# Splitting a 2048-point column transform as 32x64 in place of 16x128, inside a TensorE-bound kernel

## Chip, cores and metric

The kernel runs on one core of one Trainium2 chip. The metric is device time in microseconds (us) of that core, as the median of several executions. The kernel before took 1284.75 us (three runs, 1283.58 to 1288.89).

## The reference, cut to what matters

The kernel computes the output below and the gradients of eight of its inputs (nine outputs in all).

```python
def _A_ref(x, w_r, w_i):                      # S = 2048, D = 1024, Df = 513
    X = jnp.fft.rfft2(x.astype(jnp.float32), axes=(-2, -1))
    X = X * (w_r + 1j * w_i)
    return jnp.fft.irfft2(X, s=(S, D), axes=(-2, -1)).astype(jnp.bfloat16)

def _B_ref(x, w1, b1, w2, b2):                # F = 3584
    r = relu(einsum("bsd,df->bsf", x, w1) + b1)
    return einsum("bsf,fd->bsd", r * r, w2) + b2

g = sigmoid((x * gate_w).sum(-1, keepdims=True))
out = g * _A_ref(x, ...) + (1 - g) * _B_ref(x, ...)
# and the vector-Jacobian product with grad_out, for everything but B_x
```

Two real sequences go through the two-dimensional transform together: `x` and the gradient that flows into the spectral branch (index `T` in the code). The rest is matmuls of the MLP in bf16.

## The kernel before

The two-dimensional transform is a side job. Its generators `yield` after a piece of work, and a helper threads these pieces between groups of 16 MLP matmuls, so that TensorE always has something to do. In the traces TensorE runs its matmuls in one fixed order: while one waits (4.65 us in the step shown below), none of those behind it passes.

The transform over the 2048 rows is split in two factors, and the longer one is what the change rewrites. Before, it is a 128-point stage: a complex product with a 128x128 matrix, done as three real products (the third one on the sum of the two parts), with the common term added afterwards. This is the forward half of a step, for one of the two sequences:

```python
def spectrum(fb, m, z, mats, x):
    # ... pm = sums and differences of z; sums = re + im   (VectorE)
    for j in range(2):
        re, im = main[j]
        px = fps.tile([P, 2, H], FP32, ...)            # PSUM, H = 512
        ps = tps.tile([P, H], FP32, ...)               # PSUM
        mm(px[:, 0, :], lhsT=mats[:, j, 1, :], rhs=im, ...)
        mm(px[:, 1, :], lhsT=mats[:, j, 2, :], rhs=re, ...)
        mm(ps[:],       lhsT=mats[:, j, 0, :], rhs=sums[:, j], ...)
        common = fb.tile([P, H], FP32, ...)
        nc.scalar.copy(                                 # L328
            out=common[:].rearrange("p (i g) -> p i g", g=4),
            in_=ps[:].rearrange("p (g i) -> p i g", g=4))
        V(out=x[:, j, :, 0:H].rearrange("p c (i g) -> p c i g", g=4),        # L331
          in0=px[:].rearrange("p c (g i) -> p c i g", g=4),
          in1=common[:]..."p (o i g) -> p o i g"..., op=ALU.add)
        yield
```

The two rearranged views undo an ordering: column `g*128+i` of PSUM goes to column `i*4+g` of `x`.

The way back (`back`) has the same three products with a second matrix, ScalarE's copy of the common term, and additions on VectorE. Between the two stand the products with the spectral weights `w`. Each of the 8 steps covers a pair of the 16 long-row transforms.

Of the kernel before, what the change touches and what calls it, by code (L numbers as in the profile page):

```python
# [10 lines left out]
P = 128  # L11
# [9 lines left out]

class Geo:

    def __init__(self, S, D, F):
        assert S % P == 0 and D % P == 0 and F % P == 0
        self.S, self.D, self.F = S, D, F
        self.S2 = S // P
        assert P % self.S2 == 0
        self.Df = D // 2 + 1
        self.DC = D // P  # L30
        self.DW = min(512, D)
        assert D % self.DW == 0
        self.DCH = D // self.DW
        self.FC = F // P
        self.FGW = 512 if F % 512 == 0 else F
        assert F % self.FGW == 0 and self.FGW % P == 0
        self.FG = F // self.FGW
        self.FGC = self.FGW // P
        self.SB = 4
        assert self.S2 % self.SB == 0  # L40
        self.NSB = self.S2 // self.SB


def build_consts(g: Geo):
# [8 lines left out]
    t, pl = q // 8, q % 8  # L53
    same = (pl[:, None] == pl[None, :]).astype(np.float64)

    cc = np.arange(16)
    k2 = np.where(cc <= 8, cc, cc - 8)
    ang = tp * ((np.arange(16)[:, None] * k2[None, :]) % 16) / 16
    kf = np.where(cc[None, :] <= 8, np.cos(ang), -np.sin(ang))
    c["kf"] = (kf[t][:, t] * same).astype(FDT_NP)  # L60
    ki = np.where(cc[None, :] <= 8, np.cos(ang), np.sin(ang)).T
    c["ki"] = (ki[t][:, t] * same).astype(FDT_NP)
# [30 lines left out]
    pp = np.arange(P)  # L93
    A = np.zeros((P, S2, 3, P))
    B = np.zeros((P, S2, 3, P))
    for k in range(S2):
        th = tp * ((pp[:, None] * (k + S2 * pp[None, :])) % S) / S
        A[:, k, 0, :], A[:, k, 1, :], A[:, k, 2, :] = np.cos(th), np.sin(th) - np.cos(th), -np.cos(th) - np.sin(th)
        th = th.T
        B[:, k, 0, :], B[:, k, 1, :], B[:, k, 2, :] = np.cos(th), np.sin(th) - np.cos(th), -np.cos(th) - np.sin(th)  # L100
    c["amat"] = (A * XS).astype(FDT_NP)
    c["apmat"] = B.astype(FDT_NP)
    c["sel"] = np.tile(np.eye(32, dtype=np.float32), (4, 1))
    sg = np.ones((P, 2, 2, 2))
    sg[:, 1, 1, :] = -1.0
    c["sgn"] = sg.astype(np.float32)
# [20 lines left out]
def kernel(  # L127
# [30 lines left out]
    S2, DC, FC = g.S2, g.DC, g.FC  # L158
    NT = S // P
# [31 lines left out]
    kf = pers.tile([P, P], FDT, name="kf", tag="kf")  # L191
# [10 lines left out]
    z_scr = [dram.tile([S2, P, D], FDT, name=f"z_scr{T}") for T in range(2)]  # L202
    y_scr = [dram.tile([S2, P, D], FDT, name=f"y_scr{T}") for T in range(2)]
# [40 lines left out]
    def row_stage(fb, f, kmat, earlier=None):  # L244
# [3 lines left out]
        for b, (row, o) in enumerate(even + odd):  # L248
            first_ = mm(pk[:, b, :], lhsT=f[:, row, o], rhs=kmat, start=True, stop=True)
# [6 lines left out]
    def first_columns(fb, cf, T, i, ft, earlier=None):  # L256
# [6 lines left out]
        nc.scalar.copy(  # L263
            out=u[:].rearrange("p (h b r) -> p b h r", h=2, b=2)[:, 0], in_=pu[:, 0, :].rearrange("p (h r) -> p h r", h=2)
        )

        uv = u[:].rearrange("p (g c i) -> p g c i", g=4, c=2)
        X, Y = (w[:, :, x].rearrange("p c g i -> p g c i") for x in range(2))
        V(out=uv[:, 1::2, :, 0 : P // 2], in0=X, in1=Y, op=ALU.add)
        V(out=uv[:, 3::-2, :, P - 1 : P // 2 - 1 : -1], in0=X, in1=Y, op=ALU.subtract)  # L270
        st(out=z_scr[T][:].rearrange("c (p i) l -> i (c p) l", i=S2)[i], in_=u[:])
# [18 lines left out]
    def pair(m):  # L290
        return (m, S2 - m) if m else (0, S2 // 2)

    def rows2(ap, m):
        ka, kb = pair(m)
        return ap.rearrange("(k1 k2) l -> k1 k2 l", k2=S2)[:, ka : kb + 1 : kb - ka, :]

    def pair_mats(fb, name, m):
        ka, kb = pair(m)
        t_ = fb.tile([P, 2, 3, P], FDT, name=name, tag=name, bufs=2)
        ld(out=t_[:], in_=cten[name].ap()[:, ka : kb + 1 : kb - ka])  # L300
        return t_

    def zg(ap):
        return ap.rearrange("p (g c i) -> p c g i", g=4, c=2)

    def spectrum(fb, m, z, mats, x):

        if m:
            pm = fb.tile([P, 4, 4, P], FDT, name="pm", tag="pm")
            R, I = zg(z[:, 0]), zg(z[:, 1])[:, ::-1]  # L310
            V(out=pm[:, 2:0:-1], in0=R, in1=I, op=ALU.add)
            V(out=pm[:, 0::3], in0=R, in1=I, op=ALU.subtract)
            main = [(pm[:, 0], pm[:, 1]), (pm[:, 2], pm[:, 3])]
            re_, im_ = pm[:, 0::2], pm[:, 1::2]
        else:
            main = [(zg(z[:, j])[:, 0], zg(z[:, j])[:, 1]) for j in range(2)]
            re_, im_ = (z.rearrange("p j (g c i) -> p c j g i", g=4, c=2)[:, c] for c in range(2))
        sums = fb.tile([P, 2, 4, P], FDT, name="sums", tag="sums", bufs=2)
        V(out=sums[:], in0=re_, in1=im_, op=ALU.add)
        for j in range(2):  # L320
            re, im = main[j]
            px = fps.tile([P, 2, H], FP32, name="px", tag="ps2", bufs=2)
            ps = tps.tile([P, H], FP32, name="pxs", tag="tr", bufs=2)
            mm(px[:, 0, :], lhsT=mats[:, j, 1, :], rhs=im, start=True, stop=True)
            mm(px[:, 1, :], lhsT=mats[:, j, 2, :], rhs=re, start=True, stop=True)
            mm(ps[:], lhsT=mats[:, j, 0, :], rhs=sums[:, j], start=True, stop=True)
            common = fb.tile([P, H], FP32, name="common", tag="common", bufs=2)
            nc.scalar.copy(  # L328
                out=common[:].rearrange("p (i g) -> p i g", g=4), in_=ps[:].rearrange("p (g i) -> p i g", g=4)
            )  # L330
            V(  # L331
                out=x[:, j, :, 0:H].rearrange("p c (i g) -> p c i g", g=4), in0=px[:].rearrange("p c (g i) -> p c i g", g=4),
                in1=common[:].rearrange("p (o i g) -> p o i g", o=1, g=4).to_broadcast([P, 2, P, 4]), op=ALU.add,
            )
            yield

    def real_columns(fb, m, z, mats, xs, sgn):

        ed = fb.tile([P, 2, 2, 2, 2], FDT, name="ed", tag="ed", bufs=2)
        zc = z[:].rearrange("p t c l -> p c t l")[:, :, :, 0 : P + 1 : P]  # L340
        G = nc.gpsimd
        sp = tps.tile([P, 2, 2, 4], FP32, name="sp", tag="tr", bufs=2)
        if m:

            G.tensor_tensor(out=ed[:, 0, 0], in0=zc[:, 0], in1=zc[:, 1], op=ALU.add)
            G.tensor_tensor(out=ed[:, 0, 1], in0=zc[:, 1], in1=zc[:, 0], op=ALU.subtract)
            G.tensor_copy(out=ed[:, 1, 0], in_=zc[:, 1])
            G.tensor_scalar(out=ed[:, 1, 1], in0=zc[:, 0], scalar1=-1.0, scalar2=None, op0=ALU.mult)
            src = [[ed[:, a].rearrange("p c t l -> p (c t l)") for a in range(2)]] * 2
        else:  # L350

            ed0 = fb.tile([P, 2, 4, 4], FDT, name="ed0", tag="ed0")
            G.memset(ed0[:], 0.0)
            G.tensor_copy(out=ed0[:, :, 0, :].rearrange("p j (t l) -> p j t l", t=2), in_=zc)
            for a in (1, 3):
                G.tensor_scalar(
                    out=ed0[:, :, a, :].rearrange("p j (t l) -> p j t l", t=2), in0=zc, scalar1=-1.0, scalar2=None, op0=ALU.mult
                )
            src = [[ed0[:, j, a : a + 2, :].rearrange("p a b -> p (a b)") for a in (0, 2)] for j in range(2)]
        for j in range(2):  # L360
            o = sp[:, j].rearrange("p c b -> p (c b)")
            mm(o, lhsT=mats[:, j, 0, :], rhs=src[j][0], start=True, stop=False, skip_group_check=True)
            mm(o, lhsT=mats[:, j, 1 + j, :], rhs=src[j][1], start=False, stop=True, skip_group_check=True)
        for T in range(2):
            V(out=xs[T][:, :, :, 0::H], in0=sp[:, :, :, 2 * T : 2 * T + 2], in1=sgn[:], op=ALU.mult)

    def back(fb, m, ys, mats):

        vs = []
        for T in range(2):  # L370
            y = ys[:, T]
            v = fb.tile([P, 2, 2, LW], FDT, name="v", tag="v", bufs=2)
            sums = fb.tile([P, 2, H], FDT, name="ysums", tag="sums", bufs=2)
            V(out=sums[:], in0=y[:, :, 0, 0:H], in1=y[:, :, 1, 0:H], op=ALU.add)
            for j in range(2):
                pv = fps.tile([P, 2, H], FP32, name="pv", tag="ps2", bufs=2)
                ps = tps.tile([P, H], FP32, name="pvs", tag="tr", bufs=2)
# [37 lines left out]
    def fft_mid():  # L415
# [4 lines left out]
        def inputs(m):  # L420
            z = fb.tile([P, 2, 2, D], FDT, name="z", tag="z", bufs=2)
            for T in range(2):
                ld(out=z[:, T], in_=z_scr[T][:].rearrange("c p l -> p c l")[:, m : m + 9 : 8, :])
# [847 lines left out]
```

## Time and profile before

The prediction below shows the busy shares, two waits, the windows over the stage and its timeline. The stage is recognised in the trace by its neighbours:

| first start, us | kernel before |
|---|---|
| first MLP gradient matmul (`pw`), start of the stage | 446.1 |
| first `pki`, the way back over the rows begins | 790.3 |
| first `acc`, the stage is over | 893.6 |
| end of the profiled execution | 1283.3 |

### The profile page before, as it was taken

The numbers are of one execution on the slowest core, as the hardware profiler recorded it, in microseconds if no ns is written. First come the engines' busy times: TensorE is split into PE (matmuls) and PEld (weight loads), VectorE is DVE, ScalarE is ACT, GpSimd is POOL, SyncE is SP. The second block draws the span as 40 slices with busy tenths as digits, with TensorE's granted clock in tenths as the row PEclk, the third lists the DMA queues.
The fourth block names the chain that finished last, engine by engine and source line by source line (L and its number), as shares of the span: only waits on it lengthen the run. The fifth ranks groups of instructions, "written<-read, shape, count | busy, mean of one in ns | idle before, by whom it ended". The sixth has DMA issues, their size and how long they took to land.

```text
span 1283.3 us, 18045 instructions
## 1 busy us (share of the span) xinstructions
PE 1270.6 (99%) x6948; PEld 615.1 (48%) x6948; DVE 739.5 (58%) x1563; ACT 440.5 (34%) x736; POOL 187.0 (15%) x335
## 2 busy tenths in 40 slices
PE   8999999999999999999999999999999999999998
PEld 5555544555544444444444444555454454344443
DVE  3554433444481246686567854444877777886664
ACT  4656654666633323332333323443111121111110
POOL 0111111111100121221212222122010011000000
PEclk9999999999999999999999999999999999999999
DMA  9566353546344678898787589995899887656550
GB/s 290 199 181 183 130 156 124 180 150 193 105 129 118 158 233 194 242 214 222 180 178 180 132 151 277 292 214 185 221 217 225 197 202 207 174 152 177 149 154 33
DMA packets 314416, 234.20 MB, mean 182 GB/s; under 512 B 183852, under 2 KB 263754, under 8 KB 314330
## 3 DMA queue, kind: packets, MB, share of 16 engines
q1 hardware_dynamic: 284944, 142.19, 47.1%
q0 software_dynamic: 24576, 82.43, 18.7%
q10 hardware_dynamic: 4810, 8.43, 2.3%
q8 instruction: 54, 0.88, 0.3%
q14 instruction: 32, 0.26, 0.1%
HBM read 107.16 MB, written 81.81 MB: 147 GB/s over the span
## 4 chain that ended last, share of the span: by engine, by line
PE 60%; DVE 5%; DMA 2%; issue 2%; SPq 1%; POOL 1%; ACT 0%; POOLq 0%; DVEq 0%; ACTq 0%
PE pw L804 14%; PE acc L876 13%; PE pw L788 9%; PE xX L976 7%; PE xV L976 4%; PE pd L657 3%; PE ph L647 3%; PE xZ L976 2%; DMA z<-z_scr 2%; PE pui L282 1%; PE pki L503 1%; SPq L167 1%; DMA out_dram<-wo 1%; PE pvs L380 1%; PE pv L378 0%
## 5 line engine op out<-in xcount | busy, mean ns | idle before, releaser
L647 PE MATMUL ph<-xT,w1g 128*128 128x512 bf16 x896 | 221.1, 379 | 1.2 <-DMA w1g<-in_B_w_dram 1.2
L657 PE MATMUL pd<-dbT,w2T 128*128 128x512 bf16 x896 | 211.3, 379 | 0.4 <-DVE dhT L661 0.4
L804 PE MATMUL pw<-grp,res 128*128 128x512 bf16 x896 | 202.2, 379 | 0.0
L788 PE MATMUL pw<-dbn,grp 128*128 128x512 bf16 x896 | 201.1, 379 | 0.0
L876 PE MATMUL acc<-w,hblk 128*128 128x512 bf16 x896 | 198.7, 379 | 0.0
L661 DVE SCALAR_TENSOR_TENSOR dhT<-pd,rT 128x512 bf16<-128x512 f32 x112 | 77.4, 692 | 208.7 <-PE pd L657 156.4
L657 PEld LDWEIGHTS <-w2T 128*128 128x128 bf16 x896 | 87.1, 98 | 103.4 <-issue 1.2
L788 PEld LDWEIGHTS <-grp 128*128 128x128 bf16 x896 | 86.8, 98 | 102.6
L876 PEld LDWEIGHTS <-hblk 128*128 128x128 bf16 x896 | 86.4, 98 | 98.3
L804 PEld LDWEIGHTS <-res 128*128 128x128 bf16 x896 | 86.0, 98 | 97.8 <-issue 0.2
L647 PEld LDWEIGHTS <-w1g 128*128 128x128 bf16 x896 | 84.6, 98 | 90.4 <-DMA w1g<-in_B_w_dram 1.5
L649 ACT ACTIVATE rT<-ph,b1col 128x512 bf16<-128x512 f32 x112 | 76.9, 687 | 116.2 <-PE ph L647 116.2
L792 ACT CAST wo<-pw 128x512 bf16<-128x512 f32 x56 | 32.8, 585 | 140.3 <-PE pw L788 137.0
L809 ACT CAST wo<-pw 128x512 bf16<-128x512 f32 x56 | 32.8, 586 | 131.7 <-PE pw L804 97.1
L650 ACT ACTIVATE h2T<-rT 128x512 bf16<-128x512 bf16 x112 | 70.5, 629 | 2.5
L942 ACT ACTIVATE g<-gatew_bc,dsc 128x1024 f32<-128x1024 bf16 x16 | 18.3, 1148 | 150.7 <-DVE gxo L985 124.5
L976 PEld LDWEIGHTS <-dS 128*128 128x128 f16 x448 | 43.8, 98 | 52.8
L331 DVE TENSOR_TENSOR x<-px,common 128x1024 f16<-128x1024 f32 x32 | 38.8, 1220 | 48.8 <-ACT common L328 45.0
L505 ACT CAST rt<-pki 128x1024 f16<-128x1024 f32 x32 | 32.5, 1014 | 96.7 <-PE pki L503 88.7
L976 PEld LDWEIGHTS <-hblk 128*128 128x128 bf16 x336 | 33.1, 99 | 44.7 <-issue 3.3
L877 DVE SCALAR_TENSOR_TENSOR ot<-acc,omg,af 128x512 bf16<-128x512 f32 x32 | 24.0, 749 | 49.9 <-PE acc L876 49.7
L976 PE MATMUL xX<-dT,dS 128*128 128x512 f16 x224 | 51.0, 379 | 0.0
(201 smaller groups left out, 1517.7 us busy)
## 6 DMA issues: line engine op xcount, KB each, us to landing
h2T_scr<-h2T POOLq DMA_DIRECT2D x28, 512.0 KB, 4.4
dhT_scr<-dhT POOLq DMA_DIRECT2D x28, 512.0 KB, 4.8
hblk<-h2T_scr SPq DMA_DIRECT2D x8, 1792.0 KB, 9.8
hblk<-dhT_scr SPq DMA_DIRECT2D x8, 1792.0 KB, 8.7
z_scr<-u POOLq DMA_DIRECT2D x32, 256.0 KB, 2.9
z<-z_scr SPq DMA_DIRECT2D x16, 512.0 KB, 5.1
y_scr<-pc POOLq DMA_DIRECT2D x16, 512.0 KB, 6.5
r<-y_scr ACTq DMA_DIRECT2D x32, 256.0 KB, 4.8
```

The source lines that it names most:

```text
L331: V(out=x[:, j, :, 0:H].rearrange("p c (i g) -> p c i g", g=4), in0=px[:].rearrange("p c (g i) -> p c i g", g=4), in1=common[:].rearrange( ...
L647: mm(ph[:], lhsT=w1g[:, dc, fc % 2 * P : (fc % 2 + 1) * P], rhs=xT[:, dc, ss], start=(dc == 0), stop=(dc == DC - 1))
L649: nc.scalar.activation(rT[:], ph[:], ACT.Relu, bias=b1col[:, fc : fc + 1])
L650: nc.scalar.activation(h2T, rT[:], ACT.Square)
L657: mm(pd[:], lhsT=w_[:, ec, fc % FGC * P : (fc % FGC + 1) * P], rhs=dbT[:, ec, ss], start=(ec == 0), stop=(ec == DC - 1),)
L661: return STT(out=dhT, in0=pd[:], scalar=2.0, in1=rT[:], op0=ALU.mult, op1=ALU.mult, accum_out=gb1part[:, fc, sb : sb + 1],)
L788: mm(pw[:], lhsT=cur[:, t, fb_ * P : (fb_ + 1) * P], rhs=dbn[:, t, hf * H : (hf + 1) * H], start=(t == 0), stop=(t == NT - 1),)
L792: last = nc.scalar.copy(out=wo[:, hf * H : (hf + 1) * H], in_=pw[:])
L804: mm(pw[:], lhsT=xr[t][:, d_ * P : (d_ + 1) * P], rhs=cur[:, t, :], start=(t == 0), stop=(t == NT - 1),)
L809: nc.scalar.copy(out=wo[:], in_=pw[:])
L876: turn["PE"] = mm(acc[:], lhsT=cur[:, fc, t2 * P : (t2 + 1) * P], rhs=w2[:, fc, cs], start=(fc == 0), stop=(fc == FC - 1))
L976: mm(acc[:], lhsT=lhs[:, fc, :], rhs=rhs[:, fc, :], start=start and fc == 0, stop=fc == KH - 1, skip_group_check=True,)
```

## The change

The intent is to take matmuls out of a stream that TensorE bounds. With a factor of 64 in place of 128, a complex 64-point transform fits one 128x128 matrix with the real and the imaginary part stacked on the partitions: one matmul does what needed three, on half as many points. 192 matmuls of 512 columns become 128. The rest follows from this: 16 steps in place of 8, the edge columns (0 and 512) read once ahead of all steps, results that must be brought from the other 64 partitions, and weights `w` with a negated copy.

The core of the diff:

```diff
-    def spectrum(fb, m, z, mats, x):
-        ...three matmuls per j, common, V(...)   (shown above)
+        def transform(m, z):
+            if m:
+                pm = fb.tile([P, 2, 2, H], FDT, name="pm", tag="pm")
+                V(out=pm[:, 0], in0=z[:, 0], in1=z[:, 1], op=ALU.add)
+                V(out=pm[:, 1], in0=z[:, 0], in1=z[:, 1], op=ALU.subtract)
+            else:
+                pm = z
+            x = fb.tile([P, 2, 2, LW], FDT, name="x", tag="x", bufs=2)
+            for n in range(2):
+                px = fps.tile([P, 2, H], FP32, name="px", tag="ps2", bufs=2)
+                for T in range(2):
+                    mm(px[:, T, :], lhsT=am[:, m, n, :], rhs=pm[:, n, T, :], start=True, stop=True)
+                for c in range(2):
+                    nc.scalar.copy(
+                        out=x[lanes[n], c, :, 0:H].rearrange("p t (i g) -> p t g i", g=4),
+                        in_=px[lanes[c]].rearrange("p t (g i) -> p t g i", g=4),
+                    )
+                yield x
+        def products(x, w):
+            G.tensor_scalar(out=w[:, 2, 0:W1], in0=w[:, 1, 0:W1], scalar1=-1.0, ...)   # GpSimd
+            V(out=xw(t1_), in0=xw(x), in1=w[:, 0:1, 0:W1]..., op=ALU.mult)
+            V(out=t2_[...], in0=x[...], in1=wi, op=ALU.mult)
+            yield
+            for n in (1, 0):
+                V(out=y[lanes[0], n, ...], in0=t1_[L, 0, ...], in1=t2_[L, 1, ...], op=ALU.subtract)
+                V(out=y[lanes[1], n, ...], in0=t1_[L, 1, ...], in1=t2_[L, 0, ...], op=ALU.add)
+            yield y
+        def back(m, y):
+            for n in (1, 0):
+                for T in range(2):
+                    mm(pv[n][:, T, :], lhsT=bm[:, m, n, :], rhs=y[:, n, T, 0:H], start=True, stop=True)
+                # n == 1: ScalarE copies pv[1] to vc; n == 0: two sums on VectorE to pc
+                yield
+            # edges, stores of pc
+        for m in range(NM):                      # 16 steps
+            for x in transform(m, z):
+                yield
+            G.tensor_copy(out=x[:, :, :, 0::H], in_=ex[:, m])     # edge columns
+            for y in products(x, w):
+                yield
+            yield from back(m, y)
+            grads_of_w(m, x)
+            yield
```

## The prediction

> **What bounds the kernel now.** I read the page's busy shares first, then the 40 slices, then the waits of TensorE alone, then the windows over the stage that is rewritten, then its timeline and its groups with the shapes kept apart.
>
> ```profile
> PE 1270.6 (99%) x6948; PEld 615.1 (48%) x6948; DVE 739.5 (58%) x1563; ACT 440.5 (34%) x736; POOL 187.0 (15%) x335
> ...
> PEclk9999999999999999999999999999999999999999
> ...
> PE xX L976 <- DVE dT L971: 2.7, 1, 2.7
> PE ph L647 <- DMA w1g<-in_B_w_dram: 1.2, 1, 1.2
> ...
> 460.00:660.00 200.00, 199.30 (x956) 89.93 (x955) 137.72 (x196) 60.86 (x94) 44.40 (x85) 1.00 0.82 208
> 660.00:790.00 130.00, 129.72 (x622) 58.73 (x621) 84.52 (x125) 38.69 (x60) 30.37 (x59) 1.00 0.75 168
> ```
>
> The first line: TensorE is busy 99% of the span. A busy share alone can hide stalls, so the waits matter more: the nine entries of TensorE add up to 8.2 us, and the largest two (shown) lie at the tail and in the first stage. The windows (length, then busy time of PE, PEld, DVE, ACT, POOL, then clock, DMA share, GB/s) cover the middle of the two-dimensional transform, the stage that is rewritten: TensorE idles 0.70 us of 200 and 0.28 of 130. There the transform is a side job, threaded between groups of 16 matmuls of the MLP gradients (pw). So in this stage time is TensorE's instruction stream, and the change is worth what it takes out of that stream, less any wait it puts in.
>
> How long is a matmul in the stream? The 379 ns that the groups give is the latency of one; the timeline gives the pitch:
>
> ```profile
> 525.57 0.38 PE L378 MATMUL pv<-y,apmat 128*128 128x512 f16 x1
> 525.78 0.38 PE L379 MATMUL pv<-y,apmat 128*128 128x512 f16 x1
> 526.00 0.38 PE L380 MATMUL pvs<-ysums,apmat 128*128 128x512 f16 x1
> 526.21 3.62 PE L788 MATMUL pw<-dbn,grp 128*128 128x512 bf16 x16
> 529.67 0.38 PE L378 MATMUL pv<-y,apmat 128*128 128x512 f16 x1
> ...
> 513.81 0.17 PE L362 MATMUL sp<-ed,amat 128*128 128x8 f16 x1
> 513.84 0.17 PE L363 MATMUL sp<-ed,amat 128*128 128x8 f16 x1
> ```
>
> Starts go from 526.21 to 529.67 over 16 matmuls: 216 ns each; the three transform matmuls before them take 0.64 us, 213 ns each. So a 512-column matmul costs 0.216 us, with a new stationary operand every time; an 8-column one 0.03 us.
>
> [...]
>
> **The change part by part.** Before, the stage has 8 steps over pairs of the 16 long-row transforms. A complex product with real and imaginary parts apart is done with three real 128x128 matmuls; per step 2 inputs x 2 of the pair x 3 = 12 forward and 12 back, 24 x 8 = 192 matmuls of 512 columns. After, there are 16 steps over pairs of 32; one stationary 128x128 matrix does a complex 64-point transform of both parts, so per step 2 of the pair x 2 inputs = 4 forward and 4 back, 8 x 16 = 128. Removed: 64.
>
> TensorE: 64 x 0.216 = **13.8 us out**. Small edge matmuls: before 4 + 4 per step, 64; after 32 in one block at the start and 2 per step back, 64 again: 0. Row stage (kf, ki): 8 blocks of 128 columns per tile as before; only which half of the constant is the moving operand changes: 0. Column stage: unchanged. MLP: unchanged.
>
> VectorE, per new step: two sums for pm at 0.69 us (1.38), two products of 2052 elements at 1.24 (2.48), four combinations of 1026 elements at 0.69 (2.76; half the lanes cost no less), two sums from PSUM at 1.22 (2.44), edges 0.34, weight gradients 2 x 0.69 + 2 x 0.42 + 0.17 (2.39): 11.8 us, x16 = 189. Before, the rows of this stage (x 38.8, v 38.7, t 59, y 22, pm 19, pc 19, sums 21, gs 11, small ones 10) sum to some 240. About 50 us leave VectorE. ScalarE: four casts from PSUM of 1024 elements in each lane at 1.01 (the rt row's mean), one more for the way back, gw 0.96: 6.0 x 16 = 96 against 8 x (8 x 0.59 + 1.92) = 53; with the split cast in the first stage (two fixed costs of some 0.2 instead of one, x32 = 6) about 50 us more. Neither engine sets the end: ScalarE would be near 46% of a step (6.0 + 5.3 casts of wo at 0.59, over 20 us).
>
> GpSimd and queues: stores per 20 us step are 4 of y and 4 of gw, at the 0.72 to 0.73 of their rows some 6 us, plus about 2 for small copies and the negated weights: 8 of 20. SP issues 8 loads per step at about 0.45 (z's median issue): 3.6 us. The pair matrices go from 16 transfers of 192 KB to 2 of 1 MB. All this lies beside the matmuls.
>
> A step is now 7 pieces. The mixing rate goes from 129/110 to 145/110 side pieces per group, so a step spans 7/1.318 = 5.3 groups of 16, 5.3 x 3.45 + 8 x 0.216 + 0.1 = 20 us; 16 such are 322 us against the 8 x 41 = 330 of now. The stage keeps its place and ends some 8 us sooner; the rest of the 13.8 appears where the later pieces are mixed in. Sum: 1284.75 - 13.8 = **1271.0 us** without new waits.
>
> **Rivals.**
> *(1) The edge gather becomes a wait.* The new edges are read once, ahead of everything, from the scratch as single 2-byte elements: 8 transfers of 64 x 16 elements plus one of 64 x 4 = 8448 elements. The fast queue of now moved 284944 packets in 47.1% of 16 x 1283 us, 34 ns per packet; if elements cost as much, 8448 x 34 / 16 = 18 us, an estimate. They stand behind 2 MB of matrices (some 8 us at the 272 GB/s of this window), and the stage's loads start at 446.3, just as its MLP gradients do:
>
> ```profile
> 446.31 0.35 SPq L418 DMA_DIRECT2D sgn<-c_sgn  x1
> 446.70 0.94 SPq L423 DMA_DIRECT2D z<-z_scr  x2
> ...
> 456.48 0.38 PE L324 MATMUL px<-z,amat 128*128 128x512 f16 x1
> ```
>
> So the edges land near 475, while the first transform matmul stands at 456 and its edge matmuls at 473 now. If the 32 new edge matmuls are placed for an earlier landing, TensorE, which takes them in order, waits. For: nothing but pw covers it. Against: the order seen is not that of the source (one sums product is moved behind a pw matmul at 505.98), so placement follows expected readiness. I give one such wait of 5 to 15 us about one chance in four, which makes 1276 to 1286.
>
> *(2) The shorter step is too short for its chain.* From the last forward matmul to the first one back: two casts 2.0, edge copy 0.5, two products 2.5, two combinations 1.4, hops 0.7: 7 us, against three pieces, mostly two or three groups, 6.9 or 10.4 us. For: it is at the brink. Against: now the same chain has eight operations on VectorE (7.7 us by its rows) after 1.8 us of eviction, and TensorE waits 0.6 us in all (pvs, pv), because pw matmuls fill the gap. If it bites, 0.5 us in 16 steps, 8 us: 1279.
>
> *(3) GpSimd or the DMA becomes the bound.* Twice as many z and y row pieces of 1 KB in the outer stages, four times the stores per unit of time on GpSimd. Against: GpSimd 8 of 20 us. DMA is at 0.82 now; with buffers two deep a late z costs TensorE only if it is over 10 us late. I expect 0 to 3 us.
>
> *(4) Relief of VectorE pays more than the matmuls.* It can't: TensorE waited under 1 us for it in this stage. This caps the gain near 15 us, 1.2%.
>
> **Range and chances.** The expected waits are 0.25 x 9 for (1), and a little under 1 for (2) and (3), of which most is inside the rounding: +1.5 to +3 on 1271.0. I predict 1272.5 us. Low: all 64 matmuls and 1 us of old waits gone, 1270, less 3 for the spread of the runs before (1283.6 to 1288.9): 1267. High: a gather wait of the middle size or the chain's wait: 1283. Faster by over 2% would be below 1259.1, twice what the matmuls hold: 0.02. Slower by over 2% would be above 1310, some 39 us of new waits, more than the gather's estimate twice over: 0.03. Within 2%: 0.95.
>
> **What would show it right or wrong.** Right: TensorE's matmuls go from 6948 to about 6884, its busy time falls by some 14 us to about 1257, its waits stay under 12 us, VectorE falls by about 50 and ScalarE rises by about 50. Rival 1: an entry with sp or ed in TensorE's waits, one long gap between 450 and 480, perhaps a dip in the clock. Rival 2: px, pv waiting on y in many small entries. Rival 3: z or w landing as releaser of pm. The prediction is wrong if TensorE's pitch is not 216 ns in the new steps, or if busy time falls but the span does not.

## More of the kernel before

What the prediction did not show are the two instructions that carry the reordering, from the groups with the shapes kept apart (line, engine, operation, out<-in, shapes, count, then total us and mean ns of one, then the idle time before them and what ended it):

```profile
L331 DVE TENSOR_TENSOR x<-px,common 128x1024 f16<-128x1024 f32 x32 | 38.8, 1220 | 48.8 <-ACT common L328 45.0 <-DMA w<-in_A_w_r_dram 3.8
L383 DVE TENSOR_TENSOR v<-pv,common 128x1024 f16<-128x1024 f32 x32 | 38.7, 1219 | 4.1 <-ACT common L382 4.0
L328 ACT COPY common<-pxs 128x512 f32<-128x512 f32 x32 | 18.8, 587 | 5.0 <-PE pxs L326 3.7
L382 ACT COPY common<-pvs 128x512 f32<-128x512 f32 x32 | 18.6, 585 | 10.5 <-PE pvs L380 9.8
```

L331 and L328 reorder, while L383 and L382 do the same work on the way back without reordering. They cost the same (1220 and 1219 ns, 587 and 585 ns), so in the kernel before the reordering is free.

## The result, and the profile after

The changed kernel took **1378.82 us** (median of four, 1378.13 to 1378.94) against 1284.31 us before: ratio 1.0727, 95% interval 1.0701 to 1.0752, slower. A ratio here is the mean time of one kernel's fast runs over that of the other's in the same rounds, so it is not quite the ratio of the quoted medians. The prediction was 1272.5, "within 2%" with 0.95.

The page after, busy shares and granted clock:

```profile
PE 1283.7 (93%) x6754; PEld 616.7 (45%) x6884; DVE 697.4 (51%) x1522; ACT 581.7 (42%) x793; POOL 271.8 (20%) x456
...
PEclk9999999999999998999899899899999999999999
```

The matmuls are gone (6884 weight loads against 6948; some of the matmul records are missing), yet TensorE is busy for 13 us more, not 13.8 less, and the granted clock (the share of TensorE's full clock that it is given) dips. TensorE's waits (what waited, for what: us in total, times, longest):

```profile
PE pv L394 <- DVE y L385: 45.8, 10, 4.6
PE pw L778 <- ACT wo L782: 12.0, 5, 3.3
PE pw L794 <- ACT wo L799: 6.5, 2, 3.3
PE pki L493 <- DMA r<-y_scr: 6.5, 1, 6.5
```

Four waits hold 70.8 us; all of TensorE's waits before were 8.2. The first matmul of the way back waits for the products of its own step, 4.6 us at a time. The windows over the stage, in the same columns as before:

```profile
460.00:660.00 200.00, 167.46 (x738) 72.65 (x751) 90.40 (x142) 117.31 (x90) 74.67 (x122) 0.91 0.68 167
660.00:870.00 210.00, 176.02 (x742) 75.77 (x756) 89.86 (x133) 116.77 (x90) 76.24 (x136) 0.91 0.54 127
```

TensorE idles 32.5 us of the first 200, and the granted clock is 0.91. ScalarE, which was to be at 46% of a step, is at 59%. The stage now runs from 446.3 to 983.4 where it ran to 893.6, so nearly all of the loss lies in it. One step, from the timeline (start, length; in brackets the idle time before and its releaser), TensorE first, then ScalarE, then VectorE and GpSimd:

```profile
535.47 0.60 PE L364 MATMUL px<-pm,am 128*128 128x512 f16 x2
535.90 7.07 PE L778 MATMUL pw<-dbn,grp 128*128 128x512 bf16 x32
547.62 1.03 PE L394 MATMUL pv<-y,bm 128*128 128x512 f16 x2 [4.65 <-DVE y L385]
548.45 5.67 PE L778 MATMUL pw<-dbn,grp 128*128 128x512 bf16 x15
...
532.31 4.93 ACT L366 CAST x<-px 64x1024 f16<-64x1024 f32 x2
...
537.88 4.91 ACT L366 CAST x<-px 64x1024 f16<-64x1024 f32 x2
...
543.15 1.23 DVE L377 TENSOR_TENSOR t<-x,w 128x2052 f16<-128x2052 f16 x1 [5.76 <-POOL x L455]
544.30 1.23 DVE L379 TENSOR_TENSOR t<-x,w 128x2052 f16<-128x2052 f16 x1
545.44 0.69 DVE L434 TENSOR_TENSOR g<-x 128x1026 f16<-128x1026 f16 x1
546.16 0.69 DVE L384 TENSOR_TENSOR y<-t,t 64x1026 f16<-64x1026 f16 x1
546.87 0.70 DVE L385 TENSOR_TENSOR y<-t,t 64x1026 f16<-64x1026 f16 x1
...
542.92 0.20 POOL L455 COPY x<-ex 128x8 f16<-128x8 f16 x1 [4.17 <-ACT x L366]
```

The last forward matmul ends at 536.07. Its two casts run from 537.88 (ScalarE was still busy with the two casts before them and an eviction) to 542.79, GpSimd's edge copy follows, then two products, one product of the weight gradient that stands in between, and two combinations; `pv` starts at 547.62. That is a chain of 11.55 us against 7.07 us of cover (32 matmuls). After the wait, 15 matmuls take 5.67 us where 16 took 3.62: the granted clock is 0.5 for 6.8 us, from 545.8, still inside the wait, to 552.6. The window over it shows a mean clock of 0.69:

```profile
545.00:556.00 11.00, 8.32 (x27) 3.31 (x29) 6.95 (x12) 2.66 (x3) 5.88 (x9) 0.69 0.46 115
```

The trace has 16 such stretches in the stage, of 3.4 or 6.8 us each (78 us at half clock); the kernel before has one in the whole run (3.4 us from 1113.8, after a wait of 2.7 us). And the cast:

```profile
L366 ACT CAST x<-px 64x1024 f16<-64x1024 f32 x64 | 156.8, 2450 | 3.4 <-PE px L364 2.5 <-issue 0.2
L495 ACT CAST rt<-pki 128x1024 f16<-128x1024 f32 x32 | 32.5, 1017 | 97.9 <-PE pki L493 93.3 <-DVE rf L486 4.2
```

I had priced L366 from the `rt` row: same element count, same types. It takes 2.45 us, not 1.01. What differs is the number of partitions (64) and the walk.

### The profile page after: what moved, and what is told of

The parts are those of the page before. It is cut to its first block, busy times and chain, and to the rows that moved or that the text cites. A ratio compares the mean times of both kernels' runs of the same rounds, so it can differ in the third digit from the quotient of the medians.

```text
span 1377.1 us, 18208 instructions
## 1 busy us (share of the span) xinstructions
PE 1283.7 (93%) x6754; PEld 616.7 (45%) x6884; DVE 697.4 (51%) x1522; ACT 581.7 (42%) x793; POOL 271.8 (20%) x456
## 4 chain that ended last, share of the span: by engine, by line
PE 51%; DVE 5%; ACT 4%; issue 3%; POOL 1%; DMA 1%; another core or an unknown queue 0%; POOLq 0%; ACTq 0%; DVEq 0%
PE acc L866 12%; PE pw L794 12%; PE pw L778 10%; PE xX L966 7%; PE xV L966 3%; ACT x L366 3%; PE xZ L966 2%; PE pv L394 1%; PE pki L493 1%; PE pui L294 1%; DVE t L379 1%; PE px L364 1%; DVE y L385 1%; DVE y L384 1%; DVE g L434 0%
## 5 line engine op out<-in xcount | busy, mean ns | idle before, releaser
L778 PE MATMUL pw<-dbn,grp 128*128 128x512 bf16 x876 | 214.8, 400 | 13.5 <-ACT wo L782 12.0
L637 PE MATMUL ph<-xT,w1g 128*128 128x512 bf16 x864 | 217.0, 379 | 2.7 <-DMA w1g<-in_B_w_dram 1.2
L794 PE MATMUL pw<-grp,res 128*128 128x512 bf16 x873 | 209.7, 394 | 7.8 <-ACT wo L799 6.5
L366 ACT CAST x<-px 64x1024 f16<-64x1024 f32 x64 | 156.8, 2450 | 3.4 <-PE px L364 2.5
L778 PEld LDWEIGHTS <-grp 128*128 128x128 bf16 x896 | 91.0, 102 | 130.0 <-issue 37.9
L794 PEld LDWEIGHTS <-res 128*128 128x128 bf16 x896 | 89.2, 101 | 115.0 <-issue 23.1
L866 PEld LDWEIGHTS <-hblk 128*128 128x128 bf16 x896 | 86.4, 98 | 98.3
L495 ACT CAST rt<-pki 128x1024 f16<-128x1024 f32 x32 | 32.5, 1017 | 97.9 <-PE pki L493 93.3
L377 DVE TENSOR_TENSOR t<-x,w 128x2052 f16<-128x2052 f16 x16 | 19.7, 1232 | 106.1 <-POOL x L455 106.0
L966 PEld LDWEIGHTS <-dS 128*128 128x128 f16 x448 | 43.8, 98 | 52.9
L394 PE MATMUL pv<-y,bm 128*128 128x512 f16 x64 | 23.1, 455 | 45.9 <-DVE y L385 45.8
L283 POOL DMA_DIRECT2D z_scr<-u x32 | 22.8, 714 | 171.5 <-ACT u L278 101.6
```

Of the source, the lines that this page charges most:

```text
L366: nc.scalar.copy(out=x[lanes[n], c, :, 0:H].rearrange("p t (i g) -> p t g i", g=4), in_=px[lanes[c]].rearrange("p t (g i) -> p t g i", g=4),)
L394: mm(pv[n][:, T, :], lhsT=bm[:, m, n, :], rhs=y[:, n, T, 0:H], start=True, stop=True)
L495: nc.scalar.copy(out=rt[n][:], in_=pk[:])
L637: mm(ph[:], lhsT=w1g[:, dc, fc % 2 * P : (fc % 2 + 1) * P], rhs=xT[:, dc, ss], start=(dc == 0), stop=(dc == DC - 1))
L778: mm(pw[:], lhsT=cur[:, t, fb_ * P : (fb_ + 1) * P], rhs=dbn[:, t, hf * H : (hf + 1) * H], start=(t == 0), stop=(t == NT - 1),)
L794: mm(pw[:], lhsT=xr[t][:, d_ * P : (d_ + 1) * P], rhs=cur[:, t, :], start=(t == 0), stop=(t == NT - 1),)
```

## The experiments

All kernels gave correct results. Times are medians; "before" was between 1284.26 and 1284.90 in all groups. Versions e1, e5 to e8 and e10 to e14 have the fast walk; e2, e3, e4 and e9 have the stepped one.

| run | what it is | us (range) | ratio to before, 95% |
|---|---|---|---|
| (after) | the change | 1378.82 (1378.13–1378.94) | 1.0727 (1.0701–1.0752) |
| e1_order | casts walk so that the write is consecutive | 1302.33 (1299.85–1305.96) | 1.0138 (1.0100–1.0177) |
| e2_x32 | stepped write, `x` in float32 | 1374.63 (one run) | none |
| e3_dve | stepped cast on VectorE | 1388.54 (1387.11–1389.77) | 1.0799 (1.0768–1.0830) |
| e4_fill | stepped, 12 useless matmuls before `pv` | 1369.75 (1366.70–1371.28) | 1.0650 (1.0618–1.0683) |
| b1_stepped | kernel before with the stepped write | 1303.40 (1301.89–1306.05) | 1.0137 (1.0103–1.0172) |
| e5_early | e1, loads two steps ahead | 1310.23 (1304.34–1311.70) | 1.0173 (1.0129–1.0217) |
| e6_skew | e1, way back one step later | 1290.77 (1289.42–1295.18) | 1.0043 (1.0007–1.0079) |
| e7_both | e5 and e6 | 1293.19 (1289.42–1295.16) | 1.0052 (1.0016–1.0089) |
| e8_gap | e6, 3 empty pieces at the seam | 1289.35 (1287.14–1293.34) | 1.0033 (1.0003–1.0064) |
| e9_skewslow | e6 with the stepped write back | 1334.53 (1333.54–1336.87) | 1.0380 (1.0346–1.0413) |
| b2_split | kernel before with more, smaller stores | 1285.52 (1284.24–1289.51) | 1.0004 (0.9979–1.0029) |
| e10_queue | e7, 3 empty pieces, weight gradients stored from SyncE | 1293.97 (1289.87–1295.89) | 1.0061 (1.0037–1.0086) |
| b3_more | kernel before and 64 more matmuls | 1300.22 (1297.99–1304.74) | 1.0120 (1.0107–1.0134) |
| e11_gap7 | e6, 7 empty pieces at the seam | 1279.49 (1275.89–1282.02) | 0.9957 (0.9944–0.9971) |
| e12_wqueue | e1, `w` loaded from ScalarE's queue | 1302.68 (1298.77–1308.61) | 1.0136 (1.0091–1.0182) |
| e13_wgap | e12, 7 empty pieces at the seam | 1289.94 (1289.16–1295.01) | 1.0040 (1.0004–1.0077) |
| e14_skewgapw | e11, `w` loaded from ScalarE's queue | 1281.85 (1280.50–1282.71) | 0.9970 (0.9936–1.0004) |

### First question: why does the cast take 2.45 us?

**e1_order.** One index order in the two views; TensorE's order of instructions stays the same.

```diff
-  out=x[lanes[n], c, :, 0:H].rearrange("p t (i g) -> p t g i", g=4),
-  in_=px[lanes[c]].rearrange("p t (g i) -> p t g i", g=4),
+  out=x[lanes[n], c, :, 0:H].rearrange("p t (i g) -> p t i g", g=4),
+  in_=px[lanes[c]].rearrange("p t (g i) -> p t i g", g=4),
```

> The casts of px write the same values to the same places, but walk them so that the 2-byte results are written one after the other and the 4-byte PSUM words are read with a step of 128 instead. Instruction order on TensorE is identical to the changed kernel. Theory A (a 2-byte write with a step of 4 elements is what makes the ScalarE cast 2.45 us instead of the 1.01 predicted): casts fall to about 1.0 us, ScalarE loses about 90 us, TensorE's waits fall from 78 to under 15 us, no half-clock stretches in the stage, time 1270 to 1280. Theory B (half the lanes, or the move between lane halves, makes it slow): casts stay 2.4 us and the time stays 1379.

Measured: 1302.33 us, 76.5 less, but not the 1270 to 1280 that was expected (third question). The cast, and the waits of TensorE:

```profile
L366 ACT CAST x<-px 64x1024 f16<-64x1024 f32 x64 | 64.4, 1006 | 3.4 <-PE px L364 2.5 <-issue 0.2
```

```profile
PE pv L394 <- DVE y L385: 12.1, 9, 4.1
PE pki L493 <- DMA r<-y_scr: 6.7, 1, 6.7
```

The walk alone is worth 1.44 us per cast. The 64 partitions are not the cause: with the fast walk 64 partitions cost what 128 do (1006 ns against 1017). The waits on `wo` are gone, `pv` keeps 12.1 of 45.8, and the stretches at half clock fall from 16 to 3 in the stage (none was expected).

**e2_x32.** The tile `x` becomes float32, with the stepped write kept (`FDT` to `FP32` in its declaration).

> x kept in float32, so the cast becomes a copy that writes 4-byte elements, still 4 elements apart and to half the lanes, in the order of the changed kernel. Theory A in its narrow form (the 2-byte element is what hurts, as the copies of before wrote 4-byte elements with the same step of 4 at 0.59 us for 512): 1.0 us. If any stepped write of 1024 elements hurts, or the halves of the lanes do: about 2.4 us. VectorE's products get slower with float32 (2.1 to 2.5 us), so the time itself is not the test; the result is correct.

Measured: 1374.63 us in one look, whose state is unknown. The conclusion rests on the cast's duration:

```profile
L366 ACT COPY x<-px 64x1024 f32<-64x1024 f32 x64 | 127.1, 1986 | 3.2 <-DMA w<-in_A_w_i_dram 2.5
```

1.99 us: faster than 2.45, still twice 1.01. So a theory that only 2-byte elements suffer falls. It is the step of the write itself; why f16 suffers more than f32, and how the cost goes with steps other than four, no run shows. VectorE's products on `x` did get slower, from 1.23 us (L377 of the change) to 2.30 and 2.34. (This expectation says that the copies before wrote with a step of four. That was my misreading of their pattern; they write neighbours, as shown above.)

**e3_dve.** The stepped cast on VectorE (`nc.scalar.copy` to `nc.vector.tensor_copy`).

> The same cast with the same stepped 2-byte write, on VectorE instead of ScalarE. VectorE wrote x with this step before at 1.22 us for 1024 elements, so I expect 1.2 us each, 64 x 1.2 = 78 us more VectorE and 157 us less ScalarE. If the slow write is ScalarE's own, time falls to about 1275 to 1295; if it belongs to the destination, whoever writes it, casts take about 2.4 us and the time stays near 1379.

Measured: 1388.54 us.

```profile
L366 DVE CAST x<-px 64x1024 f16<-64x1024 f32 x64 | 157.0, 2453 | 47.9 <-PE px L364 47.0
```

2.453 us on VectorE and 2.450 on ScalarE. My expectation of some 1.2 us missed, for the same misreading: VectorE had never written with this step before. The cost belongs to the write, not to the engine.

**b1_stepped.** The opposite test: the kernel before, with the stepped walk put into its two reordering instructions.

```diff
-  out=common[:].rearrange("p (i g) -> p i g", g=4), in_=ps[:].rearrange("p (g i) -> p i g", g=4)
+  out=common[:].rearrange("p (i g) -> p g i", g=4), in_=ps[:].rearrange("p (g i) -> p g i", g=4)
   # and the same in the three views of L331
```

> The kernel before, which walks its own interleaving copies so that the written elements follow one another, made to walk them as the changed kernel does (written elements 4 apart); same values, nothing else. If the walk is what costs, and it belongs to the write whichever engine does it: common (512 float32 on ScalarE) from 0.59 to about 1.0 us, x (1024 float16 on VectorE) from 1.22 to about 2.4 us, VectorE +38 us, and the time rises, by 0 to 40 us, as the longer chain eats into the groups in between. If the changed kernel's cast was slow for its half lanes: both durations stay.

```profile
L331 DVE TENSOR_TENSOR x<-px,common 128x1024 f16<-128x1024 f32 x32 | 78.6, 2476 | 54.0 <-ACT common L328 53.6
L328 ACT COPY common<-pxs 128x512 f32<-128x512 f32 x32 | 34.4, 1094 | 15.0 <-PE pxs L326 14.1
```

1220 became 2476 ns and 587 became 1094: the slow write is made and unmade in both kernels, on both engines. It cost the kernel before 18.9 us (medians), a quarter of what it cost the new one: there it adds 32 x 1.26 + 32 x 0.51 = 56 us of work (a sum of the rows' differences) to two engines with room, here 64 x 1.44 = 92 us to ScalarE and to a chain that was at its limit.

### Second question: how does a slow cast become 76 us of TensorE time?

**e4_fill.** With the stepped cast kept, 12 useless matmuls stand before the first matmul of the way back in each step. They can start on the products and so fill part of the gap.

```diff
+ for _ in range(12 if n == 1 else 0):
+     mm(pv[n][:, 0, :], lhsT=bm[:, m, n, :], rhs=t1_[:, 0, 0, 0:H], start=True, stop=True)
```

> Slow casts kept; 12 matmuls of no use are put ahead of the first way-back matmul of each step, into the same PSUM tile that it then overwrites; they can start when the first product is done, some 3 us before the wait ends, so that TensorE is not idle long enough for its clock to be halved. Theory H (the 103 us lost in the stage are about 71 us of waits and about 30 us of half clock after them): half-clock stretches in the stage fall from 16 to at most 5, and in spite of 192 more matmuls (41 us if none were hidden) the time is equal or falls, 1350 to 1380. If the half clock costs nothing of its own, the time rises by the unhidden part, to 1390 or more.

Measured: 1369.75 us, 9 us **less** than the change, although 192 matmuls were added (192 x 0.216 = 41 us).

```profile
PE pv L394 <- DVE t L377: 14.1, 10, 1.5
...
PE pv L396 <- DVE y L385: 3.7, 9, 0.4
```

The waits for `y` of up to 4.6 us became waits of at most 1.5 us, and the stretches at half clock fell from 16 (78 us) to 4 (17 us). The waits of `pv` fell by 28.0 us (45.8 to 17.8), so 41 us of added matmuls should have cost some 13 us; instead 9 were gained, and the half clock is what else changed. So the loss has two terms, the wait and the half clock that follows it.

**e9_skewslow.** This run came later. It has the stepped write, and the way back is moved one step later (e6 below), which takes the latency of the chain off TensorE but leaves the amount of work on ScalarE.

> e6_skew, but with the slow walk of the changed kernel back in the cast (2.45 us each, nearly 10 us of ScalarE in a step of 20, 16 with its other work). If the 94 us of the changed kernel are latency, a chain too long for a fixed place in TensorE's order, the longer gap hides most of it although ScalarE does as much as in the changed kernel: 1288 to 1310. If ScalarE's amount of work is what binds, the time stays above 1340.

Measured: 1334.53 us, between the ranges of the two theories. Of the 88.0 us between the change and e6, the skew alone saves 44.3; the other half stays. The waits have changed their kind:

```profile
PE px L364 <- ACT x L366: 11.1, 9, 3.5
PE pw L804 <- ACT wo L809: 9.4, 3, 3.4
PE pki L503 <- DMA r<-y_scr: 8.1, 2, 4.4
PE pw L788 <- ACT wo L792: 6.9, 3, 3.0
PE pw L804 <- ACT wo L792: 3.0, 1, 3.0
```

With four casts of 2.45 us in a step of 20, ScalarE frees PSUM too late (`px`, `pw`). So neither "latency only" nor "ScalarE's amount only" is right. The stepped write costs 76.5 us without the skew (the change against e1) and still 43.8 us with it (e9 against e6).

### Third question: what keeps e1 above the prediction?

e1 is at 1302.3; 1271.0 was expected without new waits.

**e5_early, e6_skew, e7_both.** In e5 the loads of `z` and `w` are asked for two steps ahead (three buffers), and `w` is negated at the end of the step before. In e6 the way back of step m-1 is threaded between the forward matmuls of step m:

```diff
-        for m in range(NM):
+        for m in range(NM + 1):
-            for x in transform(m, z):
+            there = transform(m, z) if m < NM else iter(())
+            again = back(m - 1, y) if m else iter(())
+            for _ in range(2):
+                x = next(there, x)
                 yield
+                next(again, None)
+                yield
-            yield from back(m, y)
```

> e1_order with the inputs of a step asked for two steps ahead (three buffers each) and w's negation on GpSimd done a step early, out of the chain between cast and product. e1_order stayed 31 us above the forecast with 12 us of waits of pv on y, 7 of the first pki on its load, and three half-clock stretches. Theory R1 (late loads and GpSimd's queue lengthen the chain in a few steps): pv's waits fall under 4 us, half-clock stretches to at most 1, time 1280 to 1292. Theory R2 (the chain itself is too long for the gap): waits stay near 12 us, time 1298 to 1304.

> e1_order with the way back of a step put one step later, between the forward matmuls of the next, so that six pieces instead of three lie between the last forward matmul and the first one back; loads and negation as in e1_order. R2: pv's waits fall to under 2 us and the time to 1278 to 1290, with the wait of the first pki (7 us) left. R1: late loads now show as pm's or px's waits, and the time gains under 8 us.

> e5_early and e6_skew together. If nothing else is in the way than chain and loads, TensorE's waits are those of before (8 us) plus at most the pki wait (7 us): 1270 to 1282, which is the first time that the 64 removed matmuls (13.8 us) would show against the kernel before.

Measured: e5 1310.23 (no better than e1, and outside both ranges), e6 1290.77 (just above its range), e7 1293.19. In e6 no `pv` waits at all; what is left is the seam, where the last stores of this stage must land before the way back over the rows (`pki`) can read them:

```profile
PE pki L503 <- DMA r<-y_scr: 8.0, 2, 4.5
```

e7 missed its expectation and equals e6. e5 did not help, and at first I took this as proof that late loads were not the matter. The traces say otherwise. In e1 the four long waits of `pv` (3.88, 1.25, 4.08 and 1.87 us, 11.1 of 12.1) are just those steps in which GpSimd's edge copy comes straight after its negation of `w`, and that negation waits for a load. It is the negation for the next step's `w`, which stands ahead of this step's edge copy in GpSimd's order. From the timeline of e1, GpSimd and then SyncE's queue:

```profile
527.82 1.50 POOL L373 TENSOR_SCALAR w<-w 128x513 bf16<-128x513 bf16 x1 [6.21 <-DMA z<-z_scr]
529.28 0.61 POOL L789 DMA_DIRECT2D out_dram<-wo  x1
529.89 0.22 POOL L455 COPY x<-ex 128x8 f16<-128x8 f16 x1
...
508.41 11.36 SPq L177 DMA_TRANSPOSE grp<-h2T_scr  x4
519.87 0.53 SPq L785 DMA_DIRECT2D res<-in_A_x_dram  x1
520.51 0.47 SPq L320 DMA_DIRECT2D w<-in_A_w_r_dram  x1
...
523.17 1.23 SPq L320 DMA_DIRECT2D w<-in_A_w_i_dram  x2
```

The casts had ended by 526.06, but the edge copy ran at 529.89, behind the negation and a store; `w` had been issued from 520.51 to 524.40, after four transposing loads for the MLP that held the queue for 11.36 us. (Of the nine negations that wait for a load, the profile puts eight down to `w` and this one to the `z` issued right behind it.) In e5 the loads, though asked for earlier, stand behind the same transposes (its negation starts at 535.42 in the step whose `pv` waits 5.30 us), so e5 did not test this.

**e12_wqueue, e13_wgap, e14_skewgapw.** These give that theory a real test: e12 is e1 with the 64 loads of `w` issued from ScalarE's queue. e13 adds seven empty pieces at the seam, e14 does the same edit to e11 (below).

```diff
- ld(out=w[lanes[n], c_, 0:W1], in_=every(src_w, k))                  # SyncE
+ nc.scalar.dma_start(out=w[lanes[n], c_, 0:W1], in_=every(src_w, k))
```

> This is e1_order (fast cast) with one edit: the 64 loads of the spectral weights w are issued from ScalarE's queue in place of SyncE's. In the trace of e1_order the four long waits of pv on y (3.88, 1.25, 4.08, 1.87 us, 11.1 of 12.1 us) are just those where GpSimd's edge copy comes straight after the negation of w, and that negation waited for a load (527.82 in the step whose pv waited at 534.61). SyncE issued those loads at 520.51 to 524.4, behind four transposing loads that took its queue from 508.41 to 519.77. Theory L (late load): with w off that queue the long waits go; pv waits fall from 12.1 to under 3 us, no stretch at half clock follows them, and the time falls from 1302 to 1290-1295. Then e5_early was no test of this, since its loads, asked for two steps ahead, still stood behind the same transposes. Theory C (the chain of casts, products and combinations itself is too long for two groups of 16): waits stay 8 us or more and the time stays at 1299-1306.

> e12_wqueue and seven empty pieces of the side job at the seam to the way back over the long rows (as in e11_gap7), without the skew by one step. Theory L: the wait of pki on r (6.7 us in e1_order) and its stretch at half clock go as well, and the time is that of e11_gap7, 1278-1284, so the skew was never needed once w comes in time. Theory C: 1288-1296, since the waits of pv stay.

> e11_gap7 (skew by one step and seven empty pieces) with w loaded from ScalarE's queue. In e11_gap7 no pv waited, so both theories expect the same time as e11_gap7 within 3 us, 1277-1283; what may go wrong is ScalarE's issue of 64 more transfers: if each costs it 0.5 us, 2 us per step of 20 lie on an engine that is busy 9 of 20, which should be harmless.

Measured: e12 1302.68, e13 1289.94, e14 1281.85. The waits of e12:

```profile
PE pw L778 <- ACT wo L782: 7.0, 4, 3.1
PE pki L493 <- DMA r<-y_scr: 6.4, 1, 6.4
PE sp L343 <- DVE ed L339: 3.2, 1, 3.2
PE pv L394 <- DVE y L385: 3.0, 9, 1.4
```

The waits of `pv` fell from 12.1 to 3.0 us, as the theory of the late load said: that load was their cause. The time did not move, against the expectation: ScalarE now stops at those loads (in its own row the casts `wo` stood idle 28.5 us for transfers of `w`), and `pw` waits for its evictions instead, 7.0 us. One wait has become another. In e13 `pki` no longer waits and 12.7 us go, but it stays 6 us above what the late-load theory expected, and so inside the range of theory C, with 5.1 us of waits of `pv` in 13 small pieces and 2.9 of `pw`. So both times came out as theory C said and the waits as the late-load theory did: with the fast cast and `w` in time the chain nearly fits two groups of 16 (7.1 us against 6.9, a wait of 0.2 us in such steps of e12). e6, where nothing of a step's latency is in TensorE's way, remains the better remedy: e14 is no faster than e11.

**e8_gap, e11_gap7.** Empty pieces at the seam, so that more MLP matmuls stand between the last store and `pki`: counted from the last edge matmul of the way back (`si`), 48 in e8 and 80 in e11, against 31 in e6.

```diff
  load(0), load(1)
  folded(0)
+ for _ in range(7):          # 3 in e8
+     yield
```

> e6_skew with three empty pieces at the seam between the middle stage and the last one, so that some 48 instead of 31 pw matmuls cover the path last store of y, load of r, first pki. In e6_skew that seam cost 8.0 us of pki waits and a half-clock stretch of 10.2 us (about 5 us lost). If these are the rest: pki's waits under 1 us, no half clock there, 1274 to 1280, faster than the kernel before by 0.4 to 0.8%. If the seam's wait only moves (the loads come later too), the time stays at 1287 to 1292.

> e8_gap with seven empty pieces at the seam, so that 80 in place of 48 pw matmuls (17 us) cover the 15.5 us from the last way-back matmul to the first pki. The seam's wait (4.6 us) and its half-clock stretch (6.8 us) should be gone: TensorE's waits 8 to 11 us, 1278 to 1283, under the kernel before by 0.1 to 0.5%. The forecast's 1271 stays out of reach by the 4 us longer closing of the core. If the seam isn't the rest, 1287 to 1291 as e8_gap.

Measured: e8 1289.35, where `pki` still waits 4.6 us and a half-clock stretch comes with it. Counted from the last `pv`, 47 matmuls lie before the first `pki` in e6, 48 in e8 and 96 in e11: in e8 the edge matmuls moved forward, so it hardly lengthened the cover. e11 1279.49. Its waits begin:

```profile
PE xX L978 <- DMA hblk<-dhT_scr: 2.9, 1, 2.9
PE sp L343 <- DVE ed L339: 2.0, 1, 2.0
PE pw L790 <- ACT wo L794: 1.4, 1, 1.4
```

and its busy shares read

```profile
PE 1257.7 (98%) x6884; PEld 609.6 (48%) x6884; DVE 695.5 (54%) x1522; ACT 488.7 (38%) x793; POOL 272.1 (21%) x456
```

TensorE is busy for 1257.7 us; "about 1257" had been predicted. All waits add up to 13.4 us. This version beats both kernels: the kernel before by 0.43% (0.29 to 0.56), and the change by 7%.

### Controls and the closing

**b3_more** doubles one matmul per product in the kernel before: 64 redundant ones.

> The kernel before with the third product's matmul of each pair member done twice (64 more 512-column matmuls, the very number that the change removes; the second writes the same values over the first). The forecast's first step says 64 x 0.216 = 13.8 us on the path: 1298 to 1299, ratio 1.010 to 1.011. If TensorE had slack that the waits don't show, less; if the matmuls cost more than their pitch (a clock stretch, a longer chain in the full stage), more, up to 1305.

Measured: 15.4 us more for 64 matmuls, 0.24 each, against 13.8 expected. In the profiled run, the slowest of the five, 5.3 us is a wait of `pw` for a load. The price of the removed matmuls was about right.

**b2_split and e10_queue** look at the end of the kernel. From the last group of `xX` to the end of the span the change and all its versions but e10 take about 4 us longer (17.3 us in e11, 13.4 before), and GpSimd's last instruction, a closing drain, takes 8.8 us in place of 3.9 in the records. b2 cuts the stores of the kernel before so that GpSimd issues 371 transfers and not 275; e10 issues the 64 stores of the weight gradients from SyncE.

> The kernel before with its stores of y and of the weight gradients cut into the pieces of the changed kernel (by lane half and by member of the pair), so that GpSimd issues 371 transfers in place of 275 and nothing else changes. In the traces GpSimd's closing drain took 3.94 us in both kernels that issue 275 and 8.8 to 8.9 us in all that issue 372. If the number of transfers makes it: a drain of 8.8 us, the span's end 4 us later than its last store's issue says, time 1287 to 1291, +0.2 to 0.5%. If something else in the changed kernel makes it: 3.9 us and 1284.

> e7_both with the three empty pieces of e8_gap, and the weight gradients' 64 stores issued by SP in place of GpSimd (308 transfers left there). By the same reading the closing drain falls to some 5.5 us and the end comes 3 us earlier: 1280 to 1288, about level with or up to 0.4% under the kernel before. If SP's queue, held by stores that wait for their data, delays loads, it shows as waits of px or pki, and the time is above 1290.

Measured: b2 1285.52, no change, with a drain of 5.57 us: the number of transfers explains some 1.6 us of the drain and no time. e10 1293.97. Its drain takes 4.18 us and its closing 13.8 us, so there the longer closing is gone, as expected, but TensorE then waits 7.1 us for an eviction in the stage and 5.6 us for the constant `ki`, so nothing is won. That both come from loads queued behind the stores on SyncE is likely, but only argued. So the weight gradients' stores on GpSimd have a part in the longer closing, and it is not the number of transfers alone (b2 issues 371 and closes in 14.1 us); what about them costs the time stays open.

## Why the prediction was wrong, point by point

**What bounds the kernel, and the price of a matmul: right.** TensorE's stream is the bound, 64 matmuls fewer, and with the waits gone TensorE is busy for 1257.7 us. b3 confirms the pitch.

**"Four casts from PSUM of 1024 elements in each lane at 1.01 (the rt row's mean)": this is the step that failed.** They cost 2.45 us, because they write elements four apart. The row that I took had the same size and types and a consecutive write. ScalarE rose by 141 us (440.5 to 581.7), not by about 50; with the fast walk it rises by 50.2 (490.7). VectorE's fall of 42 us was near the predicted 50; half the lanes did cost no less (0.69 us for 64x1026 and for 128x1026 in the change). A fixed cost of some 0.2 us is what ScalarE's copies of two and four columns took in the kernel before (204 ns); the split cast took 379 and 490 ns in place of 591. The term was mis-sized by 64 x 1.44 = 92 us of work on an engine off the bound, and it was taken to lie beside the matmuls.

**Rival 2 was the right mechanism with the wrong size.** It gave the chain 7 us against 6.9 to 10.4 of cover and 0.5 us of wait per step. The chain measured 11.55: 6.72 for the casts in place of 2.0 (the second pair also queues behind the first), 0.69 for a product of the weight gradient that I had not put in the chain, and 4.1 in place of 5.1 for the rest. The argument against it was that before as well a long chain was hidden. The cover then was no longer than now (6.8 to 10.6 us from the last forward matmul to the first one back, 32 to 48 `pw`), but that first matmul needed only the first sequence's half of the products, and these were done in time (at 518.13 for a `pv` at 520.82; in the tightest step at 477.11 for 477.17). And rival 2 left out the half clock that came with long waits, in the change with all 16 waits of 3.2 us and more in the stage.

**Rival 1 (the edge gather): did not come true.** Its estimate took the mean of packets of all sizes, 34 ns. The trace of the change has the 8448 packets of 2 bytes at 8.9 ns each, from 457.7 to 465.7 us, so the edges landed near 466 and not near 475. The edge matmuls stood at 468 and did not wait in the change; they wait 0.4 us in e1, 1.9 in e6 and at most 3.7 (e3, e14).

**Rival 3 (GpSimd or DMA as the bound): not as a bound.** GpSimd is busy for 20%. But its order mattered: a late `w` held up the edge copy behind it in e1. "Over 10 us late" was only my estimate: in the step of e1 shown above GpSimd stood idle 6.21 us for the load before its negation, the edge copy of 0.22 us came after it, and `pv` waited 3.88 us.

**Rival 4 (a cap on the gain near 15 us): holds.** e11 gains 5.

Where the 107.8 us between the forecast without new waits (1271.0) and the change (1378.8) went, as differences of medians:

| part | us | shown by |
|---|---|---|
| stepped write of the casts: waits of `pv` and `pw`, ScalarE's amount, half clock | 76.5 | after to e1 |
| latency left with the fast cast; the late `w` made 9 of the 12 us of waits of `pv` (e12), its share of the time is not shown | 11.6 | e1 to e6 |
| seam to the way back over the rows | 11.3 | e6 to e11 |
| left over: about 4 of a longer closing, the rest small waits | 8.5 | e11 to 1271.0; cause open |

Counted in the trace of the change instead: the four waits are 70.8 us, and 67.3 us of TensorE's busy time lie in stretches at half clock, which cost about half of that, 34 us (an estimate); together some 104 of the 107.8.

**What should have been seen blind.** The code of both kernels was there: one walks `p i g`, the other `p g i`. The prediction's own range, 1267 to 1283, assumed that a chain "at the brink" costs half a microsecond when it is over; the asymmetry (little to win, an amplified loss) called for a longer upper tail.

## What to carry to other kernels

Before pricing a copy from another row of the profile, compare the walk as well as the size and the types: put the step on the PSUM read and keep the write consecutive (for 1024 f16 elements ScalarE took 1.006 us so in e1 and 2.450 with the step on the write; the unstepped `rt` took 1.017). In a stream that one in-order engine bounds, lay the chain of each step beside the matmuls that cover it; move the consumer one step later and cover the seams between stages, and price a long wait with the half clock that may come with it (in the traces of the kernel before and of the change all 18 waits of TensorE of 2.7 to 6.5 us had a stretch at clock 0.5 that began between 2.2 us before their end and 1.3 us after it, and the four of 1.1 to 1.2 us had none). After an experiment that changes nothing, check in its trace that it changed what it was meant to change.
